# Causal attention and an MLP-mixer on one core: the order of the whole instruction list is replaced, and the last batch's rows are all stored in three pieces

## The chip, the cores and the metric

The kernel runs on one core of a Trainium2 chip. The metric is the device time of one execution in microseconds (us). Three executions of the kernel before took 284.76, 285.21 and 284.71 us, median 284.76.

The core's engines each work through a list of instructions of their own: PE (TensorE) multiplies matrices and loads weights beside that, DVE (VectorE) and ACT (ScalarE) read the results out of PSUM and compute element by element, POOL (GpSimd) issues most loads and clears a few buffers, SP (SyncE) issues stores. An instruction waits on semaphores until what it needs is there.

## The reference

Inputs are q, k and v of shape 8 batches x 8 heads x 576 rows x 64, and four weights: token weights 576 x 256 and 256 x 576, channel weights 512 x 1536 and 1536 x 512. All is float32; the kernel multiplies in bf16.

```
scores = (q @ k.T) / sqrt(64), only where block(row) >= block(key), blocks of 64
attn   = softmax(scores) @ v                 -> x: 8 x 576 x 512, heads side by side
h  = relu(x.T @ w_tok1) @ w_tok2 ;  u = x + h.T      (mixes the 576 rows of a batch)
h2 = relu(u @ w_ch1) @ w_ch2 ;      out = u + h2     (mixes the 512 channels of a row)
```

## The kernel before, in words

**One list of operations.** The kernel function builds a list of 1,500-odd operations with `P.add`; each has a number, the engines that may run it, what it depends on, and a function that emits its instructions (one score set on PE is eight or more matmuls, one exponential on ACT is one instruction). Nothing is emitted while the list is built. At the end `Plan.placed()` (line 72) walks through the text `ORDER` (from line 97), and every word of it says which operation comes next, on which engine, and in which PSUM banks: `202Tabef` is operation 202 on TensorE with the banks a, b, e and f. Letters behind the number: T is PE, A ACT, D DVE, P POOL, S SP. Banks a to d are the four "mm" banks, e to h the four "late" ones; before operation 202, e to h are two double banks, s and t. Since each engine works in the order of its own list, ORDER decides everything: who waits for whom, when a bank comes free, when a load is issued. It was written out by a search outside of the kernel; the costs and priorities given to `P.add` were that search's and have no effect on the instructions.

**The start.** Buffers are cleared (`init_tiles`, L339): the zeros in `wd_sb` with which PE is kept busy, and constant columns in `vals`, `w_sb` and `w1o_sb`. `raise_clock` (L356 to L376) has two kinds of matmul on those zeros whose results nobody reads: one operation of eleven, 512 columns wide (L364), and up to 37 single ones, 512 or 256 wide (L372), of which ORDER names as many as it wants. The first q and k are loaded in pieces (`load_qk`: SP at L424, POOL at L435, later ones at L417), cast by ACT where need be, and transposed by DVE (L440); the first half of k goes by SP, the second too, each cast on ACT.

**Attention** of one batch works on four heads at a time. A score set (`score_set`, L562) is eight or more matmuls into banks; ACT takes the exponential (L580, 1,024 wide from a double bank, in the first batch; L736 and L777, 512 wide). DVE or POOL copies the end of a row of scores aside and clears the barred part (L588, L599). `head_out` multiplies with v (L616) and divides on DVE (reciprocal L636, product L642); `ends_out` does so for the last 64 rows (L669, L691, L697). The v matrices carry a column of ones, so the 65th column of the product is the sum to divide by.

**Mixer.** `token_up` (L814, L818) and `first_u` or `token_mix` (L849, L862, L874, L913, L928) mix the rows; `channel_up`, `channel_up_half` (L1114) and `channel_up_fast` (L1238) multiply with the first channel weight, `first_down` (L1463) and `channel_down_fast` (L1354 to L1438) with the second. The "half" and "fast" forms save matmuls by sums of weight blocks and of activations, which DVE or ACT form and fold together again (the folds of the last stage are L1396). Each PSUM result is read out either by DVE or by ACT (`cast` L393/L395, `relu` L800/L802), as ORDER says.

**Batches overlap.** While batch b+1 is in attention, batch b is in the mixer. Rows 0 to 511 of each batch are done by batch; the last 64 rows of all eight batches are gathered into a ninth, joint batch (512 rows), which is stored at L1424. `make_identity` (L353, operation 10) builds an identity matrix on POOL for later transposes by PE.

**The last batch.** `channel_down_fast` runs for it in two groups of rows, `c0 = 0` and `c0 = 1`; in each, two rows of blocks (`row`) by two halves of the 512 columns are folded, and what is done is stored by SP or ACT (L1438):

```
pieces = [(0, 0, 2), (1, 0, 2)] if c0 == 0 else [(0, 0, 2), (1, 1, 2), (1, 0, 1)]
```

A piece is (row, first half, end half): (0, 0, 2) is 128 rows of 512 columns, 256 KB; (1, 1, 2) is 128 rows of 256 columns, 128 KB. For every batch but the last two groups of rows are done together, as the `joint` case with `c0 = 0`.

Of the kernel before, what the change touches and what calls it, by code (L numbers as in the profile page):

```python
# [27 lines left out]
class Plan:  # L28
# [69 lines left out]
    9D 8D 14S 7D 0A 15A 11S 41Ta 19P 69Tb 17P 1D 52Tb 21P 31P 25P 51Tb 65Tb 23P 29P 48Tb 56Tb 12A 27P 3D 2D 16D 20D  # L98
    18D 22D 43Tb 13D 26D 24D 105Ts 106A 98Ttbc 61Td 57Td 49Td 99A 100D 30D 63Td 118A 122Ts 70Td 123A 78Td 62Td 54Td
    102Tt 103A 45Td 28D 64Td 104D 67Td 35P 34P 50Td 33P 158Ts 159A 142Tt 143A 32P 74Td 181P 178P 101D 55Td 115Td  # L100
    68Tb 125Ts 107Tb 184P 108T 116D 117D 124D 183D 119A 162Tt 182D 160D 47Td 179D 40P 126A 59Td 37P 42Td 109D 111Td
# [4 lines left out]
    188D 273Te 189D 169D 170D 186D 277Th 173D 241Tdbca 245A 174D 271Tg 10P 274D 244A 242A 275Te 281Ta 278D 279Th  # L106
    272D 285Tg 280A 276D 195Tedcf 198A 197A 4D 282D 5D 286D 283Th 284D 310Ta 319Tg 287Th 288A 316Td 295Tc 317T 318D
    320T 196A 243A 322Th 323T 321A 199A 228Tdbeg 324A 200D 289Tf 207D 290T 232A 230A 261D 296T 297A 6D 345D 311T
    312D 231A 191P 229A 192P 301Tb 193P 262D 346P 302T 235Tcghe 239A 291A 236A 292Td 293T 233D 190P 194P 201P 344D
    304Te 294D 305T 348D 234D 298Tc 299T 347D 352P 216Td 219Tf 220D 237A 303A 217D 218D 213Tb 222Tg 306A 214D 223D  # L110
    300A 238A 215D 240D 225Tc 226D 224D 367Tdhea 370A 227D 221D 313Tb 314T 369A 255Tc 315D 373Tfgeh 246Tb 368A 247D
    376A 307Td 308T 354D 377A 256D 248D 257D 375A 91P 249Te 250D 251D 334Th 371A 360Tcbag 364A 309D 263D 374A 92P
    372D 338Te 339T 335T 349P 362A 353D 252Tb 350D 361A 351D 363A 258Ta 393Tcfgd 397A 395A 396A 93P 336T 355P 264D
    253D 259D 260D 254D 394A 426Tb 427A 406Tagfd 337D 519P 522P 409A 521D 428Tc 340T 410A 407A 520D 400Tadfb 429A
    430Tc 408A 523D 356P 325Tg 94D 341D 358P 359P 402A 524D 431D 365P 366P 404A 357P 384Tb 385D 387Tc 95D 440Td 441A
    381Te 403A 525P 386D 326T 401A 388D 534P 528P 378Tb 389D 379D 390Td 536Tcafh 540A 537A 382D 383D 391D 380D 392D
    434Te 405P 435D 529D 539A 327T 432Td 549Tbfec 433D 685P 552A 398P 399P 553A 328D 438Th 551A 423Td 424D 425D 538A
    436Tg 437D 442Tc 526D 688P 533P 329Td 443A 446Tg 444Tc 417Ta 96D 418D 531P 411Tf 330T 412D 550A 413D 530D 445A
    447A 450D 451D 439A 454Tbg 457A 694P 469Thf 472A 527D 420Tc 421D 422D 470Te 471A 331T 332D 475T 476A 419D 460T
    461D 414Tc 455Td 456A 458Th 459A 473Tb 474A 415D 416D 543Tcade 547A 701P 452D 453D 544A 535P 686D 462T 691P 463D  # L120
    464T 465D 697P 477T 479T 545A 546A 687D 532P 541P 569Tahce 570A 572A 690D 573A 700P 689D 548P 857P 478D 602Td
    603A 604Ta 605A 576Tbecd 579A 542P 571A 480D 482T 580A 97D 606Ta 483D 578A 610Tc 607D 577A 581P 612Th 574P 467T
    468A 582Tadfe 583A 585A 611D 613D 615S 566Tb 586A 557Tg 481D 484Thc 485Ta 567D 568D 448Tb 558D 466D 487D 559D
    560Te 561D 584A 554Tf 488Td 555D 556D 563Tg 564D 565D 486A 449A 608Ta 562D 699P 609D 489A 614S 490T 491A 494T
    495D 709Tegfb 713A 712A 710A 575P 590Ta 492T 711A 591D 592D 497T 498A 493D 587Tb 496D 342S 596Ta 597D 598D 499D
    715Tefhd 718A 719A 714P 588D 716A 599Tg 589D 333S 717A 503Tca 504A 600D 692D 601D 702Tedhb 706A 705A 693D 703A
    593Tf 870P 500D 704A 695D 696D 863P 505T 635Thg 620Teb 638D 623A 507Td 626T 627A 506D 641T 642A 509T 594D 595D
    501D 748Tfhec 750A 508D 511T 751A 502D 510D 616D 752A 617D 618D 512D 749A 707P 854P 708P 513T 735Tfceh 739A 738A
    514D 858D 737A 639Td 640D 619D 698P 736A 740P 855D 515T 516D 856D 636Tc 637A 643T 770Tf 644D 771D 859D 742Tcaeh
    744A 743A 729Td 746A 865D 645T 723Tf 724D 864D 725D 720Ta 646D 517S 768Tc 624Th 730D 726Tf 745A 721D 727D 722D  # L130
    731D 648T 769A 778Tc 647A 625A 728D 860P 776Ta 621Td 866P 772Tf 622A 779D 777D 780Tc 773D 649A 781A 732Ta
    871Tgdef 872A 954P 875A 733D 873A 741D 734D 774Tc 747P 861D 628T 762Ta 630T 650Tfg 653A 651Td 775D 629D 631D
    632D 753Th 874A 754D 756Tc 763D 652A 757D 764D 755D 758D 633T 634A 654Te 655D 656T 862D 657A 783S 765Th 766D
    878Tcabd 879A 782S 660T 880A 767D 661D 881A 658T 659D 759Th 882A 957P 869P 804Tcf 807A 760D 663T 761D 664A 876D
    789Teb 785D 786D 787D 788D 819Tda 822A 810T 811D 805Th 808Tg 825T 792A 795T 809A 967P 826A 883P 812T 662D 796A
    806D 813D 790Tc 791A 793Th 794A 814T 665D 815D 917Tcged 921A 799T 800D 797T 823Td 920A 867P 817T 918A 919A 798D
    818A 824D 802T 884Thceg 803D 951P 952D 877P 886A 953D 820Tf 821A 885A 829T 964P 956D 827T 828D 888A 868P 965P
    669Tfc 887A 1051P 670A 904Tdghb 905A 960P 955D 908A 898Te 906A 830D 907A 1054P 666D 909P 899D 910P 671T 832T
    833A 900D 963P 911Tegbd 914A 895Th 672D 958D 889Ta 896D 959D 1057P 890D 915A 891D 892Tf 897D 893D 894D 912A 913A
    937Tb 916P 901Te 938A 902D 903D 981Thagd 983A 934Tf 931Te 982A 962D 925Tb 801D 932D 984A 933D 935D 985A 961D  # L140
    936D 926D 927D 831A 673Ta 674D 968Tedgh 969A 966P 972A 970A 971A 922Tf 923D 924D 1060P 675T 928Tf 1065P
    1008Tbdhe 1012A 1011A 667D 676D 677T 929D 930D 1063P 1064P 1010A 975Tfheg 978A 976A 1009A 668D 979A 678D 683S
    973P 816D 1056D 679T 680D 1053D 1052D 1014Tfead 1017A 1018A 1055D 977A 980P 939Tb 940A 1016A 681T 682D 1015A
    1001Tbhda 1004A 1058D 1002A 974P 998Te 999D 1000D 1003A 989Tc 1013P 990D 518S 1005A 992Tf 993D 991D 994D 947Td
    986Te 995Th 1068Tcbgf 1070A 1069A 1072A 1071A 945Ta 1006P 1007P 987D 988D 684S 948D 1036Te 1037A 946D 1059D
    1067P 1022Ta 1075Tfcbd 1077A 1076A 1078A 1019Tg 996D 997D 1025Th 1061D 1023D 1024D 1079A 1020D 1062D 1021D
    1028Te 1034Tc 1035A 1026D 1027D 1031Ta 1108Tgdbf 1109A 1112A 1032D 1033D 1029D 1030D 834D 1046Th 1047D 1110A
    1101Taceg 1104A 1102A 1040Tf 1041D 941Td 942D 1111A 1042Te 1043D 1073D 950S 943Th 1103A 1044Tf 1105A 1066P
    1081Tdbac 1045D 944D 1085A 1084A 1270Te 1049S 1074P 1082A 1106P 1107D 1083A 1080D 1114Tcfgh 1271D 1038Ta 1039D
    1048S 1086Td 1089Te 1090D 1087D 1091D 1116A 1117A 1113P 1092Tf 1118A 1095Tb 1096D 1097D 1115A 1125Tg 1126D  # L150
    1122Te 1123D 1127D 1124D 1128Th 1129D 1131Tb 1098Tc 1088D 1093D 1099D 835D 1132D 1100D 949S 838Tag 836D 842Td
    1094D 1119Tc 839A 1050S 844T 840T 1130D 843D 846T 845D 837D 848T 847D 1120D 1268Th 1133D 1269A 849D 850T 1121D
    1153Thc 1156A 1134D 1213Tdb 1214Tf 1282Te 1215A 1135D 1216A 841D 1136D 1137D 1157Tf 1158A 1283A 851D 1272Tg
    1273D 1219T 1220D 1154Ta 1155A 1159T 1160D 852S 1168Tge 1161T 1162D 1169Ta 1217Th 1276Td 1170A 1218D 1278Ta
    1279D 1171D 1284Tf 1277D 1221T 1223T 1224D 1285A 1163T 1222D 1294Td 1295D 1183Tfa 1174T 1172Th 1186A 1189T
    1187Td 1164D 1175D 1173A 1190D 1188D 1184Tg 1185A 1176T 1177D 1226T 1227A 784S 1191T 1192D 1290Tg 1138Tbh 1141A
# [22 lines left out]
def kernel(  # L179
# [1148 lines left out]
    def channel_down_fast(b, g_done, wc2_ready, u_done, prio):  # L1328
        gt, ut = g_of(b), u_of(b)
        joint = b != B - 1  # L1330
# [12 lines left out]
        for ts in ((0, 1),) if joint else ((0,), (1,)):  # L1343
            c0, nt = ts[0], len(ts)
# [90 lines left out]
            pieces = [(0, 0, 2), (1, 0, 2)] if c0 == 0 else [(0, 0, 2), (1, 1, 2), (1, 0, 1)]  # L1435
# [151 lines left out]
```

## Time and profile before

| | before |
|---|---|
| median of three executions | 284.76 us |
| the profiled execution's own time | 285.85 us |
| its span in the profile | 284.1 us |
| granted TensorE clock, mean | 0.999 |
| busy: PE, PE weight loads, DVE, ACT, POOL | 277.7, 194.4, 242.4, 176.0, 80.2 us |
| matmuls that the profile has | 3,586 |
| chain that ended last, share of PE | 89% |
| waits of PE that the profile lists | 2.7 us |

The profile is of one execution. Its span runs from the first instruction to the last thing that ends; the execution's own time is 1.75 us more. A timeline row gives the start and the length of a stretch in us, engine, line, operation, what is written and read, how many instructions of the kind, and in brackets how long the engine was idle just before and what released it. A stretch of x matmuls is pipelined: the last of them ends some 0.2 us after the next kind may begin, so the distance from one row's start to the next says more of their cost than the length. A row of the view by windows gives the stretch, its length, and the busy time of each engine with the count of its instructions in brackets; the last three numbers are the granted TensorE clock, the share of the DMA engines' time, and GB/s.

### The profile page before, as it was taken

The page shows a single profiled execution, that of the slowest core. Times are in us where ns is not written, and L with a number is a line of the kernel's source. Part 1 is how long each engine was busy: PE and PEld are TensorE (multiplying, and loading weights), DVE is VectorE, ACT ScalarE, POOL GpSimd, SP SyncE. Part 2 cuts the span into 40 slices and gives each one's busy share as a digit, 9 for nine tenths or more (in the row PEclk, how much of TensorE's full clock was granted, in tenths as well). Part 3 has the DMA queues.
Part 4 walks back from the last instruction along what each step waited for, and adds up shares of the span by engine and source line. Part 5 has one row for each costly group of instructions (what it writes and reads, how often), then busy time and mean ns, then how long its engine had stood idle before and what let it go on. Part 6 is the DMA issues. An engine that isn't in the chain of part 4 may idle for free.

```text
span 284.1 us, 8556 instructions
## 1 busy us (share of the span) xinstructions
PE 277.7 (98%) x3586; PEld 194.4 (68%) x3586; DVE 242.4 (85%) x527; ACT 176.0 (62%) x320; POOL 80.2 (28%) x133
## 2 busy tenths in 40 slices
PE   7999999999999999999999999999999999999994
PEld 2457665567767876887777649744488755788883
DVE  4579598889999999989988999879996979889884
ACT  3697896768798666798979891244545774530000
POOL 8876563633742313092552320000000000000000
PEclk9999999999999999999999999999999999999999
DMA  8999999969959578499999827020123600012264
GB/s 158 164 166 196 189 202 206 167 88 111 147 71 166 115 134 105 76 116 87 161 98 253 71 41 96 29 66 18 37 39 71 227 0 1 2 74 95 103 152 171
DMA packets 64773, 31.74 MB, mean 112 GB/s; under 512 B 53088, under 2 KB 55904, under 8 KB 64736
## 3 DMA queue, kind: packets, MB, share of 16 engines
q0 software_dynamic: 45040, 17.64, 53.7%
q1 hardware_dynamic: 19408, 13.05, 17.7%
q8 instruction: 28, 0.46, 0.6%
q10 hardware_dynamic: 288, 0.52, 0.5%
q14 instruction: 9, 0.07, 0.1%
HBM read 35.85 MB, written 9.44 MB: 159 GB/s over the span
## 4 chain that ended last, share of the span: by engine, by line
PE 89%; DMA 6%; POOL 1%; DVE 1%; issue 1%; ACT 1%; POOLq 0%
PE mm L1372 17%; PE late L1372 9%; PE mm L1238 7%; PE late L1114 7%; PE mm L1114 7%; PE late L1238 6%; PE mm L562 5%; PE late L616 4%; PE late L562 3%; PE mm L814 3%; PE mm L616 3%; PE late L1463 3%; PE mm L1041 3%; DMA gT<-in_k_dram 2%; PE mm L913 2%; PE late L814 2%
## 5 line engine op out<-in xcount | busy, mean ns | idle before, releaser
L777 ACT ACTIVATE e_sb<-late 128x512 bf16<-128x512 f32 x85 | 48.4, 609 | 11.5 <-PE late L562 7.3
L777 ACT ACTIVATE e_sb<-mm 128x512 bf16<-128x512 f32 x83 | 47.5, 607 | 7.7 <-PE mm L562 3.3
L440 DVE STREAM_TRANSPOSE qk_sb<-qk_sb 128x288 int32<-128x288 int32 (+2 forms) x57 | 37.0, 693 | 4.5 <-ACT qk_sb L393 1.9
L469 POOL DMA_DIRECT2D vals<-in_v_dram x45 | 37.1, 838 | 7.7 <-DMA wc_sb<-in_moe_w_ch_dram 2.5
L1372 PEld LDWEIGHTS <-gT 128*128 128x128 bf16 x288 | 27.8, 98 | 4.6
L1372 PEld LDWEIGHTS <-sums 128*128 128x128 bf16 x288 | 27.8, 98 | 4.0 <-DVE gT L1354 0.4
L562 PE MATMUL mm<-qk_sb 32*64 32x320 bf16 (+6 forms) x462 | 26.8, 274 | 0.6 <-issue 0.6
L562 PEld LDWEIGHTS <-qk_sb 32*64 32x64 bf16 (+1 forms) x1024 | 16.8, 100 | 15.0 <-issue 9.8
L616 PEld LDWEIGHTS <-e_sb 128*128 128x128 bf16 x640 | 23.5, 97 | 4.4 <-issue 1.1
L562 PE MATMUL late<-qk_sb 32*64 32x320 bf16 (+6 forms) x454 | 25.2, 276 | 0.0
L1114 PEld LDWEIGHTS <-ws_sb 128*128 128x128 bf16 x192 | 18.0, 98 | 3.9 <-issue 0.9
L599 POOL MEMSET e_sb<- 64x512 bf16 (+1 forms) x22 | 11.4, 522 | 29.2 <-ACT e_sb L777 19.0
L1114 PEld LDWEIGHTS <-wc_sb 128*128 128x128 bf16 x144 | 15.5, 114 | 1.5
L1238 PEld LDWEIGHTS <-ws_sb 128*128 128x128 bf16 x96 | 9.4, 98 | 9.7
L1372 PE MATMUL mm<-wd_sb,sums 128*128 128x256 bf16 x126 | 15.6, 273 | 0.0
L616 PE MATMUL late<-vals,e_sb 128*128 128x65 bf16 x330 | 14.4, 193 | 0.0
L642 DVE TENSOR_TENSOR x_sb<-late,rinv 128x256 bf16<-128x256 f32 x33 | 13.6, 419 | 0.7
L580 ACT ACTIVATE e_sb<-sc 128x1024 bf16<-128x1024 f32 x11 | 10.8, 1030 | 5.2 <-PE sc L562 5.0
L616 PE MATMUL mm<-vals,e_sb 128*128 128x65 bf16 x310 | 13.8, 193 | 0.0
L800 ACT ACTIVATE gT<-late 128x512 bf16<-128x512 f32 x18 | 10.6, 606 | 5.0 <-PE late L1114 2.8
L393 ACT COPY late<-mm 128x512 f32<-128x512 f32 x16 | 9.2, 578 | 7.2 <-PE mm L1238 3.7
L642 DVE TENSOR_TENSOR x_sb<-mm,rinv 128x256 bf16<-128x256 f32 x31 | 12.6, 415 | 0.5
(202 smaller groups left out, 645.7 us busy)
## 6 DMA issues: line engine op xcount, KB each, us to landing
out_dram<-o_sb SPq DMA_DIRECT2D x14, 512.0 KB, 3.3
vals<-in_v_dram POOLq DMA_DIRECT2D x28, 128.0 KB, 5.3
qk_sb<-in_k_dram POOLq DMA_DIRECT2D x12, 288.0 KB, 4.9
qk_sb<-in_q_dram POOLq DMA_DIRECT2D x12, 288.0 KB, 5.1
wc_sb<-in_moe_w_ch_dram POOLq DMA_DIRECT2D x8, 192.0 KB, 7.6
wc_sb<-in_moe_w_ch_dram POOLq DMA_DIRECT2D x3, 512.0 KB, 9.2
out_dram<-o_sb SPq DMA_DIRECT2D x5, 256.0 KB, 2.0
vals<-in_v_dram POOLq DMA_DIRECT2D x15, 64.0 KB, 4.9
```

The lines of the kernel that those rows point to most:

```text
L440: nc.vector.transpose(dst[:, 0:S, :] .rearrange("p s e -> p (s e)") .bitcast(I32) .rearrange("p (a k) -> p k a", k=NB)[:, k0:k1], raw2.bit ...
L469: nc.gpsimd.dma_start(out=t[128 - p : 128, J, hs, 0:64], in_=src)
L562: nc.tensor.matmul(out=home(n)[rows, c : c + w], lhsT=kT[i][r, 64 * j : 64 * j + keys, par], rhs=qT[i][r, 64 * q : 64 * q + w, par], start ...
L580: nc.scalar.activation(dst, sc[SC.index(note["pool"])][:, :, 0:n], EXP, scale=scale)
L599: (nc.vector if o.engine == "DVE" else nc.gpsimd).memset(late_keys, 0.0)
L616: nc.tensor.matmul(out=u[:, I, 0:65], lhsT=e[:, h, c : c + 128], rhs=vt[:, J, head, 0:65], start=(J == 0), stop=(J == I),)
L642: nc.vector.tensor_tensor(out=xt[:, 0:4, 64 * head : 64 * head + 64], in0=u[:, :, 0:64], in1=ri[:, 0:4].to_broadcast([128, 4, 64]), op=MULT,)
L777: nc.scalar.activation(dst, bank_of(x), EXP, scale=scale)
L814: nc.tensor.matmul(out=ps, lhsT=w1_sb[:, c, tt : tt + 255 : 2], rhs=xt[:, c, cols], start=(c == 0), stop=False)
L1114: nc.tensor.matmul(out=bank_of(bank)[:, 256 * o_ : 256 * o_ + 256], lhsT=x(o_, m), rhs=y[:, :, m, :], start=opens, stop=m == 1, skip_group ...
L1238: nc.tensor.matmul(out=bank_of(bank), lhsT=x(m), rhs=y[:, :, m, :], start=first and m == 0, stop=m == 1, skip_group_check=not first,)
L1372: nc.tensor.matmul(out=bank_of(bank)[:, 256 * i : 256 * i + 256], lhsT=x[:, kk, 128 * i : 128 * i + 128], rhs=y[:, kk], start=first and i ...
```

## The change

Two things change. ORDER is another one from its first word to its last: the operations are the same, but for the warming matmuls of L372, of which 20 are named instead of 31 (fifteen of 512 columns and five of 256, before 21 and ten), and but for one store. PE has 494 operations instead of 505, DVE 524 instead of 527, ACT 330 instead of 321, POOL 126 instead of 128, SP 35 instead of 38; some 60 read-outs of PSUM go by ACT instead of DVE or the other way round, and banks are given out anew. In `channel_down_fast` the three pieces are now taken wherever `joint` is false, so the last batch's group `c0 = 0` is stored in three DMAs instead of two. Its additional operation shifts the numbers of those behind it by one, from 1504 on.

Among what moves: the zeros' clear (7) goes to the head of DVE's list, and the transposes of the first q and k (13, 16, 18, 20, 22) go in the order 16, 13, 20, 18, 22 (before 16, 20, 18, 22, 13). The first score set is 102 (before 105). Ahead of it stand seven L372 matmuls in both, seven of 512 columns before, four of 512 and three of 256 after; between it and 202 stand 13 (before 23), and behind 202 none (before one, 58). Two head groups (147 and 148, 151 and 152) stood ahead of 202 and stand behind it, and so do the divides of heads 109, 110 and 117 on DVE. The identity (10) stands ahead of the second token weight (81) and of the channel weights 82 to 90, but for 82. At the end, four stores of the last batch go by ACT (before none): the last one in the list, 1502, is the row 0 of `c0 = 0`; before it was 1503, on SP.

```diff
 ORDER = """
-    9D 8D 14S 7D 0A 15A 11S 41Ta 19P 69Tb 17P 1D 52Tb 21P 31P 25P 51Tb 65Tb 23P 29P 48Tb 56Tb 12A 27P 3D 2D 16D 20D
-    18D 22D 43Tb 13D 26D 24D 105Ts 106A 98Ttbc 61Td 57Td 49Td 99A 100D 30D 63Td 118A 122Ts 70Td 123A 78Td 62Td 54Td
+    14S 19P 17P 21P 31P 7D 25P 23P 0A 15A 41Ta 55Tb 11S 29P 8D 3D 27P 35P 54Tb 1D 53Tb 9D 2D 16D 50Tb 12A 43Tb 13D
+    20D 34P 18D 22D 24D 46Tb 56Tb 102Ts 33P 58Tb 32P 103A 42Tb 98Ttbc 99A 49Td 125Ts 100D 126A 30D 181P 60Td 178P
...
-    112T 120D 121D 163A 66Tc 138Ts 180D 145Tt 110D 39P 113D 144D 38P 36P 139A 135Tc 136D 114D 79P 127Ta 128T 131Tb
-    132T 133D 165Ts 80P 140D 82P 161P 53Td 141D 146A 60Td 147Td 137D 129D 130D 166A 151Tc 152T 148T 134D 46Ta 44Ta
-    202Tabef 206A 204A 205A 164D 185D 175Tg 153D 154D 155Th 149D 176D 177D 156D 58Tc 157D 267Tc 268D 150D 203A 265Tg
-    167Th 208Tcebf 266A 187P 168T 81P 88P 87P 84P 83P 171Tg 89P 210A 269Td 209A 270A 90P 172T 211A 86P 85P 212A 343P
+    202Tcefg 134D 161D 203A 164D 205A 204A 109D 117D 110D 140P 141D 167Ta 168T 208Tbdhc 169D 209A 210A 171Tf 172T
+    186D 82P 212A 170D 185D 175Ta 211A 176D 173D 187P 265Te 177D 267Tb 144D 147Ta 151Tc 174D 271Tf 189D 268A 206A
+    148T 272A 152T 188D 266A 155Tb 241Tghdf 244A 242A 245A 243A 149D 150D 153D 154D 10P 81P 156D 157D 277Ta 278D
...
-    1519D 1523S 1516T 1493D 1517D 1522S 1491D 1496T 1498T 1520T 1497D 1502S 1499D 1521D 1524S 1500T 1501D 1503S
+    1503S 1522D 1525A 1500T 1501D 1504A 1496T 1490T 1497D 1491D 1502A
 """
...
-            pieces = [(0, 0, 2), (1, 0, 2)] if c0 == 0 else [(0, 0, 2), (1, 1, 2), (1, 0, 1)]
+            pieces = [(0, 0, 2), (1, 0, 2)] if joint else [(0, 0, 2), (1, 1, 2), (1, 0, 1)]
```

More of the change, by code (lines that the diff above doesn't have):

```diff
@@ L108 @@
[L108 to L117, printed above, removed]
@@ new lines @@
+    1198Tah 1199Te 1201A 1222D 1223T 1147D 1204T 1205A 1148T 1200A 1271D 1294Td 1295A 1153Tag 1224D 1149D 1151T
+    1152D 1276Td 1277D 1156A 1157Te 1154Tb 1292Tc 1293D 1202Td 1158A 1163T 1155A 1286Tb 1164D 1203A 1206T 1208T
+    1159T 1180D 1226T 1227A 1287D 1166T 1209D 1211T 1212A 1167A 1161T 1298S 1207D 1432Tdf 1435A 1413D 1433Th 1434A
+    1210D 1417Tbc 1418Tg 1419A 1162D 1225A 1160D 1228D 1297S 1278Ta 1279D 1272Th 1273D 1281S 1229D 1230D 1438T
+    1232Tge 1414D 1236Th 1237D 1231D 1233A 1234T 1235D 1436Ta 1415D 1416D 1238T 1420A 1423T 1274Tg 1239D 1275D 1437A
```

126 lines of the change are left out of this document (66 added, 60 removed).

## The prediction

> **What bounds the kernel now.** I read the page's first two lines, then the list of PE's waits, then the busy time by stage, then the timelines of the stages in which PE is not simply full.
>
> ```profile
> span 284.1 us, 8556 instructions
> PE 277.7 (98%) x3586; PEld 194.4 (68%) x3586; DVE 242.4 (85%) x527; ACT 176.0 (62%) x320; POOL 80.2 (28%) x133
> ```
>
> ```profile
> PE mm L364 <- DVE wd_sb L339: 1.7, 1, 1.7
> PE mm L562 <- issue: 0.6, 1, 0.6
> PE mm L372 <- DVE x_sb L642: 0.2, 1, 0.2
> PE late L913 <- ACT e_sb L777: 0.2, 1, 0.2
> ```
>
> ```profile
> core 0: us, PE busy (x) PEld busy (x) DVE busy (x) ACT busy (x) POOL busy (x), PEclk, DMA share, GB/s
> 8.38:21.94 13.56, 13.56 (x233) 7.31 (x233) 9.13 (x31) 11.49 (x13) 10.89 (x20) 1.00 1.42 167
> 21.94:31.10 9.16, 8.93 (x208) 7.23 (x208) 8.72 (x27) 7.31 (x15) 6.28 (x11) 1.00 1.12 198
> 60.00:180.00 120.00, 119.17 (x1978) 89.11 (x1975) 110.06 (x260) 91.89 (x176) 42.01 (x68) 1.00 0.84 110
> ```
>
> PE is busy 98% and waits 2.7 us in all, 1.7 of it before its first matmul. So a new order can win only at the start, in PE work that computes nothing (the warming matmuls), in the last waits, and behind the last matmul; everywhere else it can only lose. In the first row of stages PE is "full" of warming matmuls: they are what can go. In 60–180 DVE is at 110.06 of 120 (92%): the second full engine, and the likeliest to turn a reordering into PE waits. I cut the stages at 21.94, where op 202 starts (the first score set of the second batch, and the first on single banks): from there PE has real work without a break.
>
> **The start: −0.57.**
>
> ```profile
> 0.84 0.17 DVE L339 MEMSET w1o_sb<- 64x128 uint32 x1 [0.84 <-PEq L1571]
> 1.33 0.27 DVE L339 MEMSET wd_sb<- 128x256 uint32 x1
> 1.66 4.88 PE L364 MATMUL mm<-wd_sb 128*128 128x512 bf16 x11 [1.66 <-DVE wd_sb L339]
> 5.05 0.15 PEld L364 LDWEIGHTS <-wd_sb 128*128 128x128 bf16 x1 [0.28 <-issue]
> 5.48 0.15 PEld L364 LDWEIGHTS <-wd_sb 128*128 128x128 bf16 x1 [0.28 <-issue]
> 3.45 1.47 ACT L393 CAST qk_sb<-gT 128x576 bf16<-128x576 f32 x2 [1.21 <-DMA gT<-in_k_dram]
> 5.29 0.48 DVE L440 STREAM_TRANSPOSE qk_sb<-qk_sb 128x160 int32<-128x160 int32 x1 [0.41 <-DMA qk_sb<-in_q_dram]
> 6.08 1.50 DVE L440 STREAM_TRANSPOSE qk_sb<-qk_sb 128x288 int32<-128x288 int32 x3 [0.31 <-DMA qk_sb<-in_q_dram]
> 6.33 2.12 PE L372 MATMUL mm<-wd_sb 128*128 128x512 bf16 x7
> 8.38 0.88 PE L562 MATMUL sc<-qk_sb 32*128 32x512 bf16 x6
> ```
>
> The clear of the zeros (wd_sb) goes first on DVE: 0.84 instead of 1.33, so PE starts at 1.17 instead of 1.66 (−0.49). A 512-wide warming matmul takes 5.48 − 5.05 = 0.43 here. Seven of them behind 6.33 end by the first score set at 8.38: two at 0.43 (to 7.18) and five at 0.22 make 1.96 of the 2.05, so the double rate begins at about 7.2. The eleven of the first group then end at 1.17 + 11 × 0.427 = 5.87. Of the seven behind them three are 256 wide now (half the time): 512, 256, 512, 256 at half rate to 7.15, then 512, 256, 512 at 0.22, 0.11, 0.22, and the 0.09 left over above: 7.81. The inputs come sooner too: the transpose of the second half of k (op 13), the last of three in the row at 6.08 (end 7.58), needs only the cast, done at 4.92, and now goes ahead of those of q, into the holes of 0.41 and 0.31 us; all are done at about 7.1. So the fills set the first score set: 7.81 against 8.38, −0.57.
>
> This takes the rate to rise at the same moment though PE starts sooner. The Trainium skill, page "TensorE: Matmul & The Clock Gate", section "Part 1: The HAM clock gate (the "warmup" mystery)", says that a free-running window of about 3.4 us decides it, so an earlier start can bring the rise a whole window forward. By that rule the fills would end first, the inputs at 7.1 would set the first score set at about 7.3, and the sum would be 0.5 lower; that is a rival below, which needs from rows only that the rate rises before 7.1.
>
> **The first stage: −1.37.** ACT sets it once the fills no longer do.
>
> ```profile
> L580 ACT ACTIVATE e_sb<-sc 128x1024 bf16<-128x1024 f32 x11 | 10.8, 1030 | 5.2 <-PE sc L562 5.0
> 9.05 1.94 ACT L580 ACTIVATE e_sb<-sc 128x1024 bf16<-128x1024 f32 x2 [4.12 <-PE sc L562]
> 13.74 1.94 ACT L580 ACTIVATE e_sb<-sc 128x1024 bf16<-128x1024 f32 x2 [0.43 <-PE sc L562]
> 18.50 3.10 ACT L580 ACTIVATE e_sb<-sc 128x1024 bf16<-128x1024 f32 x3 [0.49 <-PE sc L562]
> 8.38:21.94 13.56, 5.55 (x24) 1.69 (x23) 1.00 1.42 167
> ```
>
> Eleven exponentials of 1024 (1.94 for two, one is 1.02, so 0.92 apart) and two of 512 (0.48 apart) run from 9.05 to 21.60, 12.55 us. Back to back they are 11 × 0.92 + 2 × 0.48 + 0.10 = 11.18. The 1.37 between are pauses, of 0.43, 0.49 and 0.24 (3.10 against 2.86) and the 0.1 lost at each restart, and the rows name PE's score sets as what ACT waited for: PE was doing fills. The last row is the same window for L372 alone: 5.55 us in 24 fills, of which the first is the end of those ahead of the score set. The new order has 13 instead of 23 there, so at the same mean (0.23) PE loses 2.3 us of fills, and two heads of 0.61 (next part): from 7.81 it would take 13.56 − 2.91 = 10.65 and be done at 18.5, 1.2 us before ACT's shortest chain (7.81 + 0.67 + 11.18 = 19.66), and I take the chain as unbroken. The first set at 7.81, its exponential 0.67 later as now, 11.18, and 202 another 0.34 behind (21.94 − 21.60): 202 at 20.0 instead of 21.94. Bounds: −1.37 (no pause) and −0.45 (0.43 and 0.49 stay).
>
> **What moves behind 202: +1.11.**
>
> ```profile
> 20.91 0.77 PE L616 MATMUL mm<-vals,e_sb 128*128 128x65 bf16 x20
> 21.52 0.49 PE L372 MATMUL mm<-wd_sb 128*128 128x256 bf16 x2
> 23.23 0.27 PE L372 MATMUL mm<-wd_sb 128*128 128x256 bf16 x1 [0.23 <-DVE x_sb L642]
> 23.34 0.38 PE L814 MATMUL mm<-x_sb,w_sb 128*128 128x128 bf16 x4
> 20.95 0.75 DVE L642 TENSOR_TENSOR x_sb<-mm,rinv 128x256 bf16<-128x256 f32 x2
> 126.83 0.60 PE L1114 MATMUL late<-uT,ws_sb 128*128 128x256 bf16 x4
> 127.36 0.40 PE L562 MATMUL mm<-qk_sb 32*128 32x512 bf16 x1
> ```
>
> - Two head groups (ops 147/148 and 151/152) now stand behind 202: 21.52 − 20.91 = 0.61, real PE work, so +0.61.
> - The fill behind 202 and the wait ahead of it go: 23.34 is where the next work starts, 0.11 of fill + 0.23 of wait: −0.34.
> - ACT and DVE arrive at 202 with more left to do: the divides of heads 109, 110 and 117 now stand behind 202 on DVE, and the bank that 117 frees is the next to be taken (167, then 208, 175, 241). The stage's row leaves DVE 0.44 of 9.16 free. One divide is 0.38 (half of 0.75), two 0.75, three 1.13; I take two, since two of the three stand ahead of that bank's release. +0.75, bounds 0.38 and 1.13.
> - Groups with 65 columns (heads' ends) stand apart once more than before. Four L1114 matmuls ahead of 127.36 took 0.53, where four of 256 columns at the fill's 0.11 are 0.44, so a change of kind costs about 0.09: +0.09.
>
> **Loads: 0.** The weights' DMAs keep their order on POOL's queue; only the builder of the identity moves ahead of the second token weight and eight channel weights.
>
> ```profile
> w_sb<-in_moe_w_tok_dram POOLq DMA_DIRECT2D x1, 288.0 KB, 5.3
> 19.25 0.54 POOL L480 DMA_DIRECT2D w_sb<-in_moe_w_tok_dram  x1
> 26.65 0.20 POOL masks.py:197 MEMSET ident<- 128x128 bf16 x1
> 27.17 2.70 POOL L469 DMA_DIRECT2D vals<-in_v_dram  x3
> 26.30 0.89 PE L849 MATMUL late<-aT,w_sb 128*128 128x128 bf16 x13
> ```
>
> It holds POOL from 26.65 to 27.17, 0.5 us. The token weight of 288 KB is issued at 19.25 and lands 5.3 us later at 24.6, 1.7 before its first use at 26.30; PE comes some 0.8 us sooner, so 0.5 later still fits. Bounds 0 and 0.5; if that cover were gone, the whole 0.5 would be PE's.
>
> **The middle and the end: +0.19.** Some 60 evacuations swap ACT against DVE and every PSUM bank is assigned anew. Of the 0.64 + 0.18 us of waits left in the middle I take half away (−0.41): the pause of 0.6 has no releaser that the list names, so I have no reason to see it return or not (bounds −0.82 and 0). Against it every new order makes some bank late by part of a DVE piece:
>
> ```profile
> 280.47 0.42 DVE L1396 TENSOR_TENSOR o_sb<-mm,e_sb 128x256 f32<-128x256 f32 x1 [0.25 <-PE mm L1372]
> DMA to landing us min/median/max: 3.3/3.7/4.2
> DMA to landing us min/median/max: 4.0/4.4/4.8
> ```
>
> a fold is 0.42; I take 0.3 in all (bounds 0 and three folds, 1.26). The last two rows are the twin stores of the joint batch (L1424), first on SP's queue, then on ACT's, issued at the same moments with the same bytes: ACT's land 0.6 to 0.7 later. The new order's last store (row 0 of the first group, 256 KB) goes by ACT's queue, the old one's by SP's: +0.3, half of it, since each twin also competes with the other (bounds 0 and 0.7). That store is a whole row, so the split into three pieces is not at the end: the additional issue stands beside PE's last matmuls and costs 0. The Trainium skill, page "DMA: Bandwidth & Descriptors", section "Queues, rings and completion order", gives SP and ACT one ring each on the same 16 engines, by which the queue would make no difference and the sum would be 0.3 lower; the twins say otherwise here, and I stay with them by half.
>
> **Sum.** −0.57 − 1.37 + 0.61 − 0.34 + 0.75 + 0.09 − 0.41 + 0.30 + 0.30 = −0.64. The profiled execution took 285.85 (span 284.1), 1.09 over the median of 284.76, so it would come to 285.21, and against the median to 284.1. From no change one can tell here about 0.2%, 0.57 us: faster is below 284.19, slower above 285.33. Likeliest case's own range: 283.4 to 284.8.
>
> **Rivals.**
> - *The first stage keeps its pauses (no change).* If PE meets ACT's free score banks late again, 0.43 + 0.49 stay: 284.1 + 0.92 = 285.0. For it: all three pauses end on PE's score sets. Against it: ten fills fewer stand between them. With part of this, chance 0.27.
> - *DVE becomes the bound (slower).* Place: 60–180, where it has 9.94 us in 120 free and now gets other evacuations. Each bank that it frees late stops PE for a fold, 0.42. Three beyond those counted make 285.4, which decides; four 285.8. For it: 92% busy. Against it: DVE has three instructions fewer and ACT ten more. Chance 0.23.
> - *The rate rises early (faster).* 0.5 lower, 283.6, as the rule above has it; no row shows it, since in the only start seen the rate rose at 7.2. Chance 0.05.
> - The forecast, 284.1: 0.45.
>
> Range: the low end is the early rise with a free ACT queue and no late bank in the middle, 284.1 − 0.5 − 0.3 − 0.3 = 283.0, a little in: 283.1. The high end takes in four late folds, 285.8. That leaves out about 0.2. Faster 0.50, same 0.27, slower 0.23.
>
> **What would show it.** The first 512-wide warming matmul at 1.2 and the first score set at 7.8 (7.3 if the rate rises early); ACT's thirteen exponentials without a pause, 11.2 us long; op 202 at 20.0; PE's next waits on DVE's divides, 0.75 together; in the list of waits no "issue" of 0.6; the last store on ACT's queue. The prediction is wrong if PE's waits behind 25 us, all together, exceed 1.2 us, if ACT still pauses on score sets, or if a load appears as a releaser of PE.

## The result, and the profile after

The changed kernel takes 286.68 us (median of four, 286.36 to 286.90) against 284.77 for the kernel before: the ratio is 1.0068, with an interval of 1.0054 to 1.0083. It is 1.9 us slower, where 0.6 us less was forecast, and lies above the range. Of the executions on record, four of the twelve of one kernel below (fewer warming matmuls in the old order) had a granted clock of 0.975 to 0.979 and took 287.06 to 289.76 us, where every other one has 0.997 or more; the other eight of that kernel have a median of 284.2 us, while 284.41 is the median of all twelve, and what lowered the clock is open.

The page of the changed kernel, its list of PE's waits, and its busy times by stage (the stage from the first score set to 202, the stage behind, and the middle):

```profile
span 284.4 us, 8548 instructions
PE 278.3 (98%) x3575; PEld 194.0 (68%) x3575; DVE 242.0 (85%) x524; ACT 177.4 (62%) x325; POOL 79.0 (28%) x131
```

```profile
PE mm L364 <- DVE wd_sb L339: 1.2, 1, 1.2
PE mm L849 <- DMA w_sb<-in_moe_w_tok_dram: 0.3, 1, 0.3
PE late L562 <- DVE x_sb L697: 0.2, 1, 0.2
PE late L562 <- ACT e_sb L580: 0.2, 1, 0.2
```

```profile
7.64:19.67 12.03, 11.75 (x203) 6.42 (x203) 8.35 (x27) 11.31 (x13) 9.78 (x18) 1.00 1.50 175
19.67:31.00 11.33, 10.92 (x228) 8.30 (x228) 9.04 (x29) 9.70 (x21) 6.75 (x12) 1.00 1.07 180
60.00:180.00 120.00, 119.64 (x1962) 88.45 (x1961) 110.95 (x263) 91.09 (x176) 37.53 (x61) 1.00 0.83 112
```

The list of waits holds 0.8 us fewer waits than before and eleven matmuls fewer, and still PE is busy longer (278.3 against 277.7). So the list does not carry the loss. A matmul's end is modelled and overlaps the next, so a gap of up to some 0.2 us between two of them, and the part of each longer gap that the modelled end covers, counts as busy.

**The start went as forecast.** Rows of the timelines of DVE, PE and ACT in the changed kernel:

```profile
0.87 0.27 DVE L339 MEMSET wd_sb<- 128x256 uint32 x1 [0.87 <-PEq L1571]
1.20 4.87 PE L364 MATMUL mm<-wd_sb 128*128 128x512 bf16 x11 [1.20 <-DVE wd_sb L339]
7.64 0.63 PE L562 MATMUL sc<-qk_sb 32*128 32x448 bf16 x8
8.31 2.91 ACT L580 ACTIVATE e_sb<-sc 128x1024 bf16<-128x1024 f32 x3 [3.35 <-PE sc L562]
12.06 7.55 ACT L580 ACTIVATE e_sb<-sc 128x1024 bf16<-128x1024 f32 x8
19.67 0.38 PE L562 MATMUL late<-qk_sb 32*128 32x448 bf16 x3 [0.16 <-ACT e_sb L580]
```

PE starts at 1.20 (1.17 forecast), the first score set at 7.64 (7.81). ACT's thirteen exponentials run from 8.31 to 19.61, 11.3 us, without a pause (11.18). Op 202 has its first bank at 19.14 and the others at 19.67 (20.0), 2.3 us earlier than in the first profile of the kernel before and 1.7 earlier than in its second (21.32).

**What took it back** shows at three places. Rows of PE's timelines (matmuls, and PEld, the weight loads) and of DVE's, changed kernel:

```profile
25.88 1.51 PE L849 MATMUL mm<-aT,w_sb 128*128 128x128 bf16 x24 [0.27 <-DMA w_sb<-in_moe_w_tok_dram]
30.78 0.58 PEld L1041 LDWEIGHTS <-wc_sb 128*128 128x128 bf16 x4 [0.61 <-DMA wc_sb<-in_moe_w_ch_dram]
95.77 0.54 DVE L1086 TENSOR_TENSOR th_sb<-uT 128x512 bf16<-128x512 bf16 x1 [1.15 <-DMA uT<-u_sb]
97.77 0.22 PEld L1372 LDWEIGHTS <-sums 128*128 128x128 bf16 x3 [0.41 <-DVE sums L1354]
```

First, behind 202 PE is ahead of its inputs: it meets the second token weight (25.88) and a channel weight (30.78) as they land. The prediction had named this, a load that releases PE, as a sign of being wrong. Second, at 95.77 DVE has stood 1.15 us for a DMA transpose of rows (uT), and PE then stands 0.41 for a sum that DVE had behind that instruction. In the kernel before the same instruction stood behind these sums, and its transposes had landed by 91.3:

```profile
97.55 0.95 DVE L1354 TENSOR_TENSOR sums<-gT,sums 128x1536 bf16<-128x1536 bf16 x1
100.49 0.41 DVE L1086 TENSOR_TENSOR th_sb<-uT 128x512 bf16<-128x512 bf16 x1
```

Third, the end. SP walks there through the semaphores of the DMA queues one after another (L1582). Its instructions after the last landing, first in the kernel before (from 282.9), then in the changed one (from 283.0):

```profile
L1582 SPq EVENT_SEMAPHORE  x3: 17/17/28, 282.9 to 284.0; - x3
```

```profile
L1582 SPq EVENT_SEMAPHORE  x10: 17/28/28, 283.0 to 284.3; - x10
L1438 ACTq DMA_DIRECT2D out_dram<-o_sb x1: 339/339/339, 281.0 to 281.0; - x1
DMA to landing us min/median/max: 2.0/2.0/2.0
```

With one DMA more in the program the last store has the second semaphore of that walk, and not the last: seven further waits come behind its landing, 0.43 us (283.03 to 283.46). From the last landing to the end of the execution pass 285.85 − 282.93 = 2.92 us before and 286.49 − 283.02 = 3.47 after. The store itself lands 2.0 us after its issue on ACT's queue, as its counterpart did on SP's (280.93 to 282.93).

### The profile page after: what moved, and what is told of

Read it like the earlier page. It is cut to its first block, busy times and chain, and to the rows that moved or that the text cites. A ratio compares the mean times of both kernels' runs of the same rounds, so it can differ in the third digit from the quotient of the medians.

```text
span 284.4 us, 8548 instructions
## 1 busy us (share of the span) xinstructions
PE 278.3 (98%) x3575; PEld 194.0 (68%) x3575; DVE 242.0 (85%) x524; ACT 177.4 (62%) x325; POOL 79.0 (28%) x131
## 4 chain that ended last, share of the span: by engine, by line
PE 82%; DMA 8%; POOL 4%; DVE 3%; issue 1%; DVEq 0%; POOLq 0%
PE mm L1372 13%; PE late L1372 11%; PE late L1238 7%; PE late L1114 6%; PE mm L1114 6%; PE mm L1238 6%; PE mm L562 4%; DMA wc_sb<-in_moe_w_ch_dram 3%; PE late L562 3%; PE mm L616 3%; PE late L616 3%; PE late L1463 3%; PE mm L913 3%; DMA gT<-in_k_dram 2%; DMA uT<-u_sb 2%; PE late L1041 2%
## 5 line engine op out<-in xcount | busy, mean ns | idle before, releaser
L777 ACT ACTIVATE e_sb<-mm 128x512 bf16<-128x512 f32 x91 | 52.2, 610 | 16.0 <-PE mm L562 9.8
L777 ACT ACTIVATE e_sb<-late 128x512 bf16<-128x512 f32 x77 | 44.4, 615 | 3.0 <-PE mm L562 2.3
L393 ACT COPY mm<-mm 128x512 f32<-128x512 f32 (+1 forms) x10 | 5.6, 560 | 20.4 <-DVE o_sb L1396 10.7
L393 ACT COPY mm<-late 128x512 f32<-128x512 f32 x16 | 9.4, 590 | 12.5 <-PE late L1238 5.9
L616 PE MATMUL mm<-vals,e_sb 128*128 128x65 bf16 x360 | 15.9, 193 | 0.0
L599 POOL MEMSET e_sb<- 64x512 bf16 x19 | 9.8, 522 | 21.2 <-ACT e_sb L777 12.0
L642 DVE TENSOR_TENSOR x_sb<-mm,rinv 128x256 bf16<-128x256 f32 x36 | 14.8, 419 | 0.7
L393 ACT COPY late<-mm 128x512 f32<-128x512 f32 (+1 forms) x12 | 6.8, 563 | 10.5 <-PE mm L1114 4.7
L417 POOL DMA_DIRECT2D qk_sb<-in_k_dram x12 | 6.6, 546 | 23.5 <-DVE x_sb L642 11.0
L1372 PE MATMUL mm<-wd_sb,sums 128*128 128x256 bf16 x102 | 12.8, 273 | 0.1
```

Source lines behind the costliest of these rows:

```text
L393: nc.scalar.copy(dst, src)
L599: (nc.vector if o.engine == "DVE" else nc.gpsimd).memset(late_keys, 0.0)
L616: nc.tensor.matmul(out=u[:, I, 0:65], lhsT=e[:, h, c : c + 128], rhs=vt[:, J, head, 0:65], start=(J == 0), stop=(J == I),)
L642: nc.vector.tensor_tensor(out=xt[:, 0:4, 64 * head : 64 * head + 64], in0=u[:, :, 0:64], in1=ri[:, 0:4].to_broadcast([128, 4, 64]), op=MULT,)
L777: nc.scalar.activation(dst, bank_of(x), EXP, scale=scale)
L1372: nc.tensor.matmul(out=bank_of(bank)[:, 256 * i : 256 * i + 256], lhsT=x[:, kk, 128 * i : 128 * i + 128], rhs=y[:, kk], start=first and i ...
```

## The experiments

In kernels with a shorter text of ORDER the line numbers are two or three lower than in the two kernels compared (L1082 to L1084 is L1086, and so on). Each run is compared with executions of the kernel before taken beside it, whose median lies between 284.52 and 284.87 us; so ratios can be compared between runs, and medians only roughly.

### The two kernels profiled again

No edit.

> The kernel before, profiled a second time. Theory A (the pause of 0.83 us inside a score set at 145.28 in the first profile, which the list of waits gives to no releaser, belongs to that one execution): no such pause, and the span is about 283.0 to 283.3, as the median (284.77) less the 1.75 between span and execution says. Rival B (it belongs to the order): the pause stands at the same place and the span is 284.

> The changed kernel, profiled a second time. Theory A (loads hold PE from 25 to 52 us): the second token weight and the channel weights land again just as PE asks for them, within 0.1 us for op 83 and for the last load 93, and PE reaches the end of that stage at the same time as in the first profile, 52 us. Rival B (two of the sixteen DMA engines were late by chance in that one execution: 14 of the 16 parts of the token weight had landed by 23.94, the last two at 25.66 and 25.84): it lands by about 24.2, and the span is about 1.3 us shorter.

The kernel before came at 284.36 us with a span of 282.5. Rows of PE's timeline of that second profile, and then the same two places' rows of the first one:

```profile
span 282.5 us, 8531 instructions
1.66 4.32 PE L364 MATMUL mm<-wd_sb 128*128 128x512 bf16 x11 [1.66 <-DVE wd_sb L339]
7.76 0.88 PE L562 MATMUL sc<-qk_sb 32*128 32x512 bf16 x6 [0.27 <-DVE qk_sb L440]
144.94 0.19 PE L562 MATMUL late<-qk_sb 32*128 32x64 bf16 x2
144.96 0.19 PE L562 MATMUL mm<-qk_sb 32*128 32x64 bf16 x2
```

```profile
145.70 0.19 PE L562 MATMUL late<-qk_sb 32*128 32x64 bf16 x2
146.53 0.20 PE L562 MATMUL mm<-qk_sb 32*128 32x64 bf16 x2 [0.64 <-issue]
```

The pause inside the score set (146.53 − 145.70 = 0.83 where the second profile has 0.02) belongs to the first execution, so theory A stands; the span is shorter than it said. The first score set started 0.62 earlier as well: eleven warming matmuls took 4.32 us instead of 4.88, because the double rate began in the middle of them, and now the inputs (DVE's transposes) set the score set, no longer the fills. The two differences, 0.81 and 0.62, are 1.43 of the 1.6 us between the spans.

The changed kernel came at 287.46 us, span 285.2. Rows of PE and DVE:

```profile
25.45 0.40 PE L562 MATMUL late<-qk_sb 32*128 32x512 bf16 x2 [0.77 <-DVE rinv L636]
26.01 1.53 PE L849 MATMUL mm<-aT,w_sb 128*128 128x128 bf16 x24
96.72 0.42 DVE L1086 TENSOR_TENSOR th_sb<-uT 128x512 bf16<-128x512 bf16 x1 [2.36 <-DMA uT<-u_sb]
98.61 1.16 PE L1372 MATMUL mm<-wd_sb,sums 128*128 128x256 bf16 x9 [1.24 <-DVE sums L1354]
```

The answer lies between the two. The token weight landed at 25.53, not at 24.2. The channel weights landed up to 1.4 earlier this time (op 83 at 29.36 instead of 30.74), so part of their lateness was chance, and still PE began L849 no earlier (26.01 against 25.88), because DVE's reciprocal held a score set by 0.77. The wait at 97 grew to 1.24, and the execution is the slowest of the five.

### PE's lead taken away: nine more warming matmuls ahead of 202

```diff
-    132T 57Tc 133D 108T 202Tcefg
+    132T 57Tc 63Tc 64Tc 65Tc 67Tc 68Tc 69Tc 71Tc 72Tc 73Tc 133D 108T 202Tcefg
```

> The changed kernel with nine more 512-wide warming matmuls ahead of op 202, 1.94 us of PE time, so that 202 starts at 21.5 instead of 19.6. Theory A (what PE gains ahead of 202 it loses to loads behind it): little changes, 0 to +0.6 us. Rival B (PE loses its time to the new order from 60 us on, and nothing waits for loads): +1.9 us, 288.6.

Measured: 286.80 us, ratio 1.0071 (1.0046 to 1.0097) to the kernel before; the changed kernel has 1.0068. Rows of PE:

```profile
18.13 2.32 PE L370 MATMUL mm<-wd_sb 128*128 128x512 bf16 x9
20.60 0.38 PE L560 MATMUL late<-qk_sb 32*128 32x448 bf16 x3
26.49 1.51 PE L847 MATMUL mm<-aT,w_sb 128*128 128x128 bf16 x24
```

The nine take 2.16 us (18.13 to the matmuls behind them at 20.29), but PE had time in hand ahead of 202: it starts at 20.60, not at 21.5, which is 0.9 later than in the first profile of the changed kernel and 1.3 later than in the second (19.34). The first use of the token weight (L847, L849 above) comes 0.5 to 0.6 later than without them, and the time is the same: 0.1 us more by the ratios, with some 0.8 us of uncertainty. That is theory A for about 1 us of lead. Whether a lead of 2 us would be worth nothing is not shown.

### The start alone, in the old order

```diff
-    9D 8D 14S 7D 0A 15A 11S 41Ta 19P 69Tb ... 48Tb 56Tb 12A 27P 3D 2D 16D 20D 18D 22D 43Tb 13D 26D 24D 105Ts
+    7D 9D 8D 14S 0A 15A 11S 41Ta 19P 69Tb ... 48Tb 12A 27P 3D 2D 16D 13D 20D 18D 22D 26D 24D 105Ts
```

> The kernel before with the start of the changed one alone: the zeros are cleared first, the first transposes go in the order 16, 13, 20, 18, 22, and five 512-wide warming matmuls stand ahead of the first score set instead of seven; the rest of the order is the old one. The first score set should start at 7.6 instead of 8.38. Theory A (the loads land when they land, and the old order has 1.7 us in hand at the second token weight and 2.0 at the channel weights): the 0.7 goes through to the end, 284.0 to 284.2. Rival B (PE has no such room, every gain at the start is lost at once behind it): 284.6 to 284.9.

Measured: 284.03 us, ratio 0.9966 (0.9950 to 0.9982): faster than both kernels.

```profile
5.56 1.24 PE L370 MATMUL mm<-wd_sb 128*128 128x512 bf16 x5
6.95 0.88 PE L560 MATMUL sc<-qk_sb 32*128 32x512 bf16 x6
7.61 1.94 ACT L578 ACTIVATE e_sb<-sc 128x1024 bf16<-128x1024 f32 x2 [2.71 <-PE sc L560]
```

The first score set starts at 6.95, 0.81 earlier than in the second profile of the kernel before, 202 at 20.50 instead of 21.32, and the last matmul group at 277.06 instead of 278.05. The old order lets the gain through to the end.

### Fewer warming matmuls in the old order

On top of that, ten warming matmuls between the first score set and 202 are left out (61, 57, 49, 63, 62, 45, 64, 68, 47 and 66).

> The kernel before with the start of the changed one (as in the run before_start) and ten warming matmuls fewer between the first score set and op 202 (1.95 us of PE time), the rest of the order as it was. ACT's exponentials then set 202: 6.95 + 0.67 + 11.18 + 0.34 = 19.1 instead of 20.5. Theory A (behind 202 loads and DVE's backlog hold PE: the old order has 1.0 to 2.0 us in hand there, most of which the start has taken): about half of the 1.3 arrives, 283.2 to 283.7. Rival B (there is room for all of it): 282.7. Rival C (nothing arrives, as in the changed kernel): 284.0.

Measured: 284.41 us, ratio 0.9988 (0.9962 to 1.0014). This reads like rival C, but the run did not test what it was for:

```profile
PE sc L559 <- DVE qk_sb L437: 1.7, 2, 1.1
7.30 0.89 PE L559 MATMUL sc<-qk_sb 32*128 32x512 bf16 x6 [1.15 <-DVE qk_sb L437]
18.84 1.02 ACT L577 ACTIVATE e_sb<-sc 128x1024 bf16<-128x1024 f32 x1 [0.40 <-PE sc L559]
```

The transposes of q and k, which wait for their loads, held PE twice (1.7 us), ACT paused again, and 202 came at 20.39, 0.11 earlier than in the run before. What the old order does with a 202 at 19 is not shown. Even so it met the same load: the second token weight landed at 25.02 in this execution (24.45 in the run before), and PE first used it at 25.07.

### One DVE instruction behind two sums

```diff
-    615S 616D 706A 635Tcg 857P 638A 620Tef 623A 696D 500D 501D 506D
+    615S 706A 635Tcg 857P 638A 620Tef 623A 696D 500D 501D 616D 506D
```

> The changed kernel with one DVE instruction moved: op 616 (L1086, the difference of two blocks of the transposed rows) goes behind the two sums 500 and 501 (L1354) instead of ahead of them. In the two profiles of the changed kernel DVE stands 1.15 and 2.36 us before 616 until the DMA transpose of the rows has landed, and PE then waits 0.41 and 1.2 us for the sums behind it. Theory A (one DVE instruction that waits for a transfer, with PE's own inputs queued behind it, carries 0.4 to 1.2 of the loss): 0.3 to 1.0 us less than the changed kernel, 285.8 to 286.5. Rival B (the sums are late for other reasons, or PE meets the next late bank at once): no change, 286.7 to 286.9.

Measured: 285.50 us (twelve runs), ratio 1.0029 (1.0013 to 1.0046). The place in the trace, DVE and PE:

```profile
96.33 0.96 DVE L1351 TENSOR_TENSOR sums<-gT,sums 128x1536 bf16<-128x1536 bf16 x1
97.22 0.41 DVE L1083 TENSOR_TENSOR th_sb<-uT 128x512 bf16<-128x512 bf16 x1
97.66 1.47 PE L1369 MATMUL mm<-wd_sb,sums 128*128 128x256 bf16 x12
```

Neither DVE nor PE waits there any more. The edit gives 616 the place behind both sums that it has in the kernel before. This is theory A with a larger price than expected: 1.0068 − 1.0029 = 0.0039, 1.1 us, from one instruction's place, and the two intervals do not overlap. It is a mean: how long DVE stands there differs from execution to execution (0.71 us in the run after_81, 2.36 in the second profile above).

### The last batch's stores on SP's queue

```diff
-    1524A ... 1525A ... 1504A ... 1502A
+    1524S ... 1525S ... 1504S ... 1502S
```

> The changed kernel with the last batch's four stores on ACT's queue put on SP's, so that all of its six go by SP. Theory A (a store on ACT's queue lands later and the execution ends later behind it: in every run the changed kernel takes 2.1 to 2.2 us more than its span, the one before 1.75 to 1.85): 0.3 to 0.6 us less, 286.2 to 286.5, and the difference between time and span falls to 1.8. Rival B (the queue makes no difference): no change, 286.7 to 286.9.

Measured: 286.72 us, ratio 1.0072 (1.0048 to 1.0097): rival B. The time outside of the span stayed 2.08 to 2.23 us; it is 2.06 to 2.31 in every run with the new order, against 1.73 to 1.95 in the runs of the kernel before. The trace shows no instruction there, and the cause of these 0.3 us stays open.

### The pieces alone, and the pieces exchanged

```diff
-            pieces = [(0, 0, 2), (1, 0, 2)] if c0 == 0 else [(0, 0, 2), (1, 1, 2), (1, 0, 1)]
+            pieces = [(0, 0, 2), (1, 0, 2)] if joint else [(0, 0, 2), (1, 1, 2), (1, 0, 1)]
```

> The kernel before with the line of the pieces alone: the last batch's first rows stored in three DMAs, the last of them 128 KB instead of 256 KB, all on SP, the order otherwise as it was. Theory A (the store is split at the very end here, so it lands a little sooner): 0 to 0.3 us less, 284.5 to 284.8. Rival B (one more DMA at the end costs its issue): 0.2 to 0.5 us more.

Measured: 285.03 us (twelve runs), ratio 1.0021 (1.0002 to 1.0040), which is rival B's sign and about its size; the interval almost reaches 1. Then three pieces for `c0 = 0` and two for `c0 = 1`, so that the number of DMAs is the old one:

```diff
-            pieces = [(0, 0, 2), (1, 0, 2)] if c0 == 0 else [(0, 0, 2), (1, 1, 2), (1, 0, 1)]
+            pieces = [(0, 0, 2), (1, 0, 2)] if joint or c0 else [(0, 0, 2), (1, 1, 2), (1, 0, 1)]
```

> The kernel before with the pieces exchanged: the last batch's first rows (c0 = 0) stored in three DMAs, its second (c0 = 1) in two, so that there are as many DMAs in all as before and the last one, now 128 KB, takes the semaphore 118 again. In the traces SP goes at the end through the DMA semaphores in a fixed order, 109 second and 118 last, some 0.06 us each; with one DMA more the last store has 109, and the whole walk comes behind its landing. Theory A (this walk is what the additional DMA costs): the time comes back to that of the kernel before or 0.1 less for the smaller last store, 284.6 to 284.8, with 2.9 to 3.1 us from the last landing to the end of the execution. Rival B (it is the split of c0 = 0 itself): 285.0, as in the run before_pieces, with 3.5 to 3.7 us.

Measured: 284.23 us (twelve runs), ratio 0.9993 (0.9980 to 1.0005). SP's walk after the last landing, first with the pieces alone (from 280.95), then exchanged (from 281.25):

```profile
L1580 SPq EVENT_SEMAPHORE  x10: 17/28/28, 281.0 to 282.8; - x10
```

```profile
L1580 SPq EVENT_SEMAPHORE  x3: 17/17/28, 281.3 to 282.3; - x3
```

The split is the same in both for `c0 = 0`, whose 128 KB piece ends both kernels; what differs is the count of DMAs, and with it the walk: 284.68 − 281.0 = 3.7 us from landing to end against 284.19 − 281.3 = 2.9. Seven waits at 0.06 us are 0.43 of the 0.8 between the two; the rest lies in the steps behind the last wait and is not explained. So theory A of the second run holds, 0.0028 or 0.8 us between the two ratios, though their intervals overlap a little.

### The changed kernel without these two

Op 616 moved as above, and the old pieces (two stores for `c0 = 0`, the last one still by ACT).

> The changed kernel with op 616 behind the sums (the run after_616, 285.5) and the old pieces, two DMAs for c0 = 0; the last store stays on ACT's queue and has the semaphore 118. Theory A (the additional DMA costs 0.5 at the end by the semaphore that the last store gets): 284.9 to 285.1. Rival B (it costs nothing, as predicted): 285.5.

Measured: 284.71 us (twelve runs), ratio 1.0003 (0.9992 to 1.0015). SP has three waits behind the last landing again, as in the kernel before. The old pieces are worth 0.0026, 0.7 us, here too (the two intervals overlap by 0.0002), so theory A holds, with a little more than it said.

With the two edits the time is that of the kernel before, though 202 comes earlier. Where the rest of the gain goes, no list of waits shows. It is seen when two executions are matched by the matmuls done, the warming ones left out. The first two rows are of the old order (the run with the pieces exchanged), where 1,678 and 2,782 matmuls are done; the last two are of this run, where the same numbers of each kind are done:

```profile
113.83 0.32 PE L560 MATMUL late<-qk_sb 32*64 32x320 bf16 x1
174.75 0.71 PE L1370 MATMUL mm<-wc_sb,gT 128*128 128x256 bf16 x5
```

```profile
113.85 0.33 PE L559 MATMUL mm<-qk_sb 32*64 32x320 bf16 x3
175.50 0.71 PE L1369 MATMUL mm<-wc_sb,gT 128*128 128x256 bf16 x5
```

The same matmuls take 60.9 us in the old order (61.8 in the first profile of the kernel before, with the pause of 0.83 in it) and 61.65 in the new one, and 61.66 in the three other profiles of the new order that can be matched so (the first of the changed kernel and the two of the next section). PE goes there from the matmuls of one line to those of another 75 times instead of 71, and at these changes the distances between matmuls are longer than their shapes' mean by 6.2 us in all instead of 5.5. That makes the changes the likely cause of the 0.7 us; no run tests it.

### The identity behind the token weight's load, alone and with the rest

```diff
-    154D 10P 81P 156D
+    154D 81P 10P 156D
```

> The changed kernel with the identity's builder (op 10) behind the second token weight's load (op 81) on POOL instead of ahead of it, so that 81 is issued at 18.8 instead of 19.3. In five profiles of the changed order 81 lands at 25.4 to 26.4 and its first reader, op 277 on PE, starts 0.04 to 0.05 behind that in three of them and 0.5 behind in two; in the old order it lands at 24.1 to 24.6. Theory A (0.5 us of POOL ahead of this load sets PE's way through this stage): 81 lands 0.5 to 1.3 earlier and the time falls by 0.3 to 0.9, 285.8 to 286.4. Rival B (DVE and the other loads hold PE as well): 81 lands earlier, but the time stays at 286.6 to 286.8.

Measured: 285.97 us, ratio 1.0067 (1.0041 to 1.0092). Rows of the load and its reader:

```profile
L477 POOL DMA_DIRECT2D w_sb<-in_moe_w_tok_dram x1: 556/556/556, 18.9 to 18.9; - x1
DMA to landing us min/median/max: 5.4/5.4/5.4
25.43 1.51 PE L846 MATMUL mm<-aT,w_sb 128*128 128x128 bf16 x24
```

The weight lands at 24.2, as in the kernel before, and PE takes it up 1.2 us later, no longer waiting for it. The first use came 0.45 earlier than in the first profile of the changed kernel, and by the ratio the time is the same, which is rival B. The six executions differ by 2.5 us (285.37 to 287.91) and their median lies in theory A's range, so a gain of 0.5 us is not excluded by this run alone. The next run, which has the edit on top of the two others, shows no such gain.

> The changed kernel with all three: op 616 behind the sums, the identity behind the load of 81, the old pieces. Theory A (three separate causes): the sum of what each brings, 284.4 to 284.8, no slower than the kernel before. Rival B (the new order is late elsewhere as well, and what is mended in one place is lost in the next): 285.0 to 285.5.

Measured: 284.60 us (twelve runs), ratio 1.0003 (0.9992 to 1.0015), the same as without this move (284.71 beside it). So of the three edits two carry the whole difference of 1.9 us to the kernel before, and the third nothing that shows (0.1 us, uncertain by 0.5). The time is theory A's, though one of its three causes is none.

## Why the prediction was wrong

**The start (−0.57) and the first stage (−1.37): right** in size. ACT's chain ran without a pause. The start was in part luck: the first score set begins at 7.95 on average in the four profiles with the old start and at 7.48 in the eight with the new one, so 8.38, from which the sum set out, was late. And in eight of these twelve it waits for the inputs (DVE's transposes, 0.3 to 1.1 us), where the sum had the warming matmuls set it.

**What moves behind 202 (+1.11): the mechanism right, the size too small.** The sum let 0.8 us of the lead through. In the run with nine more warming matmuls about 1 us less of lead changed the time by 0.1 us, which is uncertain by 0.8. Matched by matmuls with the same old-order profile as above, four profiles of the new order are ahead by 1.24 to 1.47 us where 167 matmuls are done (18.88 us in the old order), by 0.28 to 1.06 at 424 (32.18) and by 0.01 to 0.78 at 1,412 (93.18). The steps that failed are "Loads: 0" and the backlog's "+0.75, bounds 0.38 and 1.13". The loads were judged by their landings in the old order (24.6 for the token weight, with 1.7 in hand and 0.5 taken off); in the new one it landed at 25.8, and PE stood before it. That is not the whole of it: with the load back at 24.2 the time was no shorter, and in the second profile DVE's reciprocal held it. That PE comes to several bounds at once here, each seen only when the others are away, is argued from these waits and not tested. How the rest of the lead divides between DVE's backlog and the loads stays open.

**The middle (+0.30, bounds 0 and 1.26): the step that cost most.** DVE was named as the full engine and the second rival had the place (60 to 180) and the sign, but the wrong mechanism. The busy time of DVE there is as before (110.95 of 120 against 110.06). It was not late for lack of time: in 80 to 100 us it was busy for 17.76 us instead of 19.26, with the sums behind an instruction that waited for a DMA transpose. The prediction looked at what DVE has to do, and not at what stands at the head of its list while a transfer is under way. That one place is 1.1 us.

**Groups that stand apart once more (+0.09): too small, as far as the traces tell.** This was counted once, behind 202. Between 114 and 175 us the new order loses 0.7 us without a listed wait, with four changes of line more; that they are the cause is not tested.

**Half of the pause (−0.41): counted twice.** The profiled execution was 1.09 us over the median, and this was taken off at the end; but the pause of 0.83 was part of the reason why that execution was slow. The order did not cause it, so there was nothing to gain.

**The last store (+0.30): nothing.** On ACT's queue the store landed 2.0 us after its issue, as on SP's, and with all stores on SP's the time was 286.72 instead of 286.68. The rule of the Trainium skill, page "DMA: Bandwidth & Descriptors", section "Queues, rings and completion order", that SP and ACT each have one ring on each of the same 16 DMA engines, agrees with the 2.0 and 2.0 us here; the twins that competed with each other were the wrong row to price it by.

**The split (0): wrong.** "The additional issue stands beside PE's last matmuls and costs 0" holds for the issue, and leaves out what comes behind the last landing. With one DMA more the last store has another semaphore, and the walk at the end is in a fixed order: 0.7 to 0.8 us by the ratios, 0.5 to 0.8 by the traces.

Together: from 284.1 the middle's place adds 1.1 − 0.3, the end 0.7 − 0.3, the pause 0.4, which makes 285.7. The other 1.0 us no run divides; by the traces it is the 0.7 us between 114 and 175 us and what was lost of the lead before that.

**The rivals.** That the first stage keeps its pauses did not happen. The early rise of the rate (0.05) is no rival but a property of each execution. From the distances of the warming matmuls (0.43 and 0.22 us for 512 columns), the double rate began within the one that starts at 7.18 and at 5.04 us in the two profiles of the kernel before, and at 6.50 and 4.59 in those of the changed one. In the last of these the first score set came at 7.32, set by the inputs, as the rival said, and the time was no lower. The Trainium skill says of its window, page "TensorE: Matmul & The Clock Gate", section "Part 1: The HAM clock gate (the "warmup" mystery)", that it runs free and that the same kernel ramps at another point from run to run; the traces agree. A number that depends on it has to be taken from more than one execution.

## What to carry to other kernels

Before you cost a new order by the busy time of its second fullest engine, look for instructions on that engine that wait for a transfer, and ask what stands behind each that PE needs soon: such an instruction belongs behind everything that does not need the transfer. A lead of the bound engine is worth something only as far as its loads and the other engines' lists are ahead as well, and the cheapest test is to take the lead away with idle work, to see in the trace how much of it is gone, and whether the time changes. Do not subtract a pause from a profile and then compare with the median: profile twice first.

## What the runs showed of the hardware that was not expected

The end of these kernels has a price that depends on which semaphore the last DMA signals: SP waits for the queues' semaphores one by one, some 0.06 us each, and what stands behind the one that lands last is added to the time. One store more moved the last one from the last semaphore to the second, 0.43 us of waits and 0.7 to 0.8 us by the ratios.

The two DMA transposes that SP issues between 80 and 100 us (L980) landed after 3.1 and 5.1 us in the kernel before and after 3.2 and 6.8 us in the changed one; 6.8 was the one for which DVE stood. In all eight profiles of the new order, where the two are issued 2.5 us apart, the second takes 6.3 to 8.0 us; in the six of the old one, 4.6 to 4.8 apart, it takes 3.1. Why is not shown.

In the fourteen profiles, whose first matmul starts at 1.2 or 1.7 us, the double rate begins within a matmul that starts between 3.7 and 7.2 us. In the two profiles of the kernel before the first score set came 0.62 us apart with it (8.38 with the late rise, 7.76 with the early one, where the inputs set it).
